# Moving every large on-chip tile to a multiple of 512 bytes, and keeping only gelu's slope, in a two-layer decode training step

## The chip, the cores and the metric

The kernel runs on one NeuronCore of a Trainium2 chip. The metric is the device time of one execution in microseconds (us); lower is better. Of the core, five instruction streams matter here: TensorE (PE, with its weight loads shown apart as PEld), VectorE (DVE), ScalarE (ACT), GpSimd (POOL) and SyncE (SP). SP and POOL issue the transfers between main memory (HBM) and the on-chip memory (SBUF); 16 DMA engines carry them out. SBUF has 128 partitions; a tile has the same byte offset in every one of them.

## The reference

Forward and backward pass of four blocks for two rows of 1,024 numbers: attention with a cached context, MLP, and the same two again with the same weights. The inputs are bfloat16.

```
def _A_ref(x, k_cache, v_cache, wq, wo):      # caches [2, 4, 16384, 128], 32 query heads, 8 to a cache head
    q = (x @ wq) in heads
    p = _softmax(q . k_cache * Dh ** -0.5)
    return (p . v_cache) in heads joined @ wo
def _B_ref(x, w1, b1, w2, b2):                # w1 [1024, 3584], w2 [3584, 1024]
    y = _layernorm(x)
    h = _gelu(y @ w1 + b1)                    # tanh form of gelu
    return h @ w2 + b2
x = A_x
x = x + _A_ref(_layernorm(x), ...)            # layer 0
x = x + _B_ref(_layernorm(x), ...)
x = x + _A_ref(_layernorm(x), ...)            # layer 1
x = x + _B_ref(_layernorm(x), ...)
```

Returned are the output and the gradients of A_x, of both caches, and of wq, wo, w1, b1, w2 and b2 for a given gradient of the output. The caches are 32 MB each and are read several times; their gradients are as large and are written once, for both layers together.

## The kernel before

**What streams.** Two rows leave almost no reuse, so the kernel is a stream of 1 MB chunks from HBM. A chunk is a slot tile of 128 partitions by 8,192 bytes: a quarter of one cache head's keys or values (8,192 bytes in a row), or four 128-row blocks of a weight matrix (four runs of 2,048 bytes), or one block of w1 (7,168 bytes). There are 14 slot tiles, and three more slots in the tile `last` until the last stage; the halves of tiles that are not yet in use (`e1`, `ds1`) serve as slots for a while.

**Order.** Pieces of work are recorded with `emit` in the order in which they are to run, each with the chunks that it uses. `Program.run` goes through them once, gives a chunk a slot as soon as one is free, issues its load on SP's queue (L288 for caches, L293 for weights) and frees the slot behind the last piece that uses it. Nothing is reordered after that: the order on each engine is the order of the pieces.

**Stages.** Attention of layer 0 (`attn_fwd`), MLP forward of layer 0 (`mlp_in`, `w1_fwd`, `gelu_fwd`, `gelu_out`, then w2), attention and MLP of layer 1, the MLP backward of layer 1, attention backward of layer 1 (`attn_bwd`), MLP backward of layer 0, attention backward of layer 0 with all the weight and cache gradients. In an attention stage PE turns 128x128 blocks of a chunk (L321), ACT or DVE copies eight turned blocks from PSUM into one of three tiles `kT` (L191, L194), and PE multiplies by them (L661 forward, L937 backward). Other blocks are used as they are loaded (L644, L918). In the last stage the gradients are made in PSUM (L1022, L1069), copied by ACT or DVE (L199, L202) into a half slot, the staging buffer, and stored by POOL (L1029, L1085) in pieces of 512 KB, 4,096 bytes to a partition.

**gelu.** `gelu_fwd` (L734 to L754) makes from the sums of w1 the tiles `hpre` (the input of gelu), `sg` (one over 1 + e^z), `gq` (1 - sg, the sigmoid) and `pl` (the polynomial in the slope), each 128 partitions by 56 numbers, 224 bytes, and keeps all four per layer in the pool `vec`. `gelu_out` makes gelu from `gq` and `hpre` for the w2 product. `gelu_slope` (L760 to L766) turns `pl` into gelu's slope with three DVE instructions:

```
        V.tensor_tensor(out=pl[:], in0=pl[:], in1=sg[:], op=ALU.mult)
        V.tensor_scalar(out=pl[:], in0=pl[:], scalar1=1.0, scalar2=None, op0=ALU.add)
        V.tensor_tensor(out=pl[:], in0=pl[:], in1=q[:], op=ALU.mult)
```

For layer 1 it is called right behind `gelu_fwd` (L1189). For layer 0 it is called in the MLP backward of that layer (L1258), ahead of the seven pieces `w2_use` and the multiplication at L1263 that needs it.

**Where tiles lie.** The pools lie one behind the other in each partition, in the order in which they are opened: `const`, `vec`, `wrk`, `small`, `ktp` (the three `kT`), `pers` (`e0`, `e1`, `ds1`, `last`, then the 14 slots). A tile's size is rounded up to 32 bytes. So a byte added to an early pool moves all that lies behind it. Adding the sizes up, the first `kT` begins at byte 32,672, the first slot at byte 114,592, and the last slot ends at byte 229,280.

Of the kernel before, what the change touches and what calls it, by code (L numbers as in the profile page):

```python
# [9 lines left out]
F32 = mybir.dt.float32  # L10
I32 = mybir.dt.int32
ACT = mybir.ActivationFunctionType
ALU = mybir.AluOpType
# [10 lines left out]
LAG_B = 13  # L24
LAG_K = 15
NSTG = 12
STG_FROM = (0, 0, 0, 4, 8, 12)


# [23 lines left out]
class Program:  # L53
# [11 lines left out]
    def emit(self, fn, uses=()):  # L65
        i = len(self.ops)
        self.ops.append((fn, tuple(uses)))
        for c in uses:
            if c.first is None:
                c.first = i  # L70
            c.last = i
# [31 lines left out]
def kernel(  # L103
# [25 lines left out]
    V = nc.vector  # L129
# [11 lines left out]
    FJ = F // 128  # L141
# [8 lines left out]
    emit = P.emit  # L150
# [5 lines left out]
    const = ctx.enter_context(tc.tile_pool(name="const", bufs=1))  # L156
    vec = ctx.enter_context(tc.tile_pool(name="vec", bufs=1))
    wrk = ctx.enter_context(tc.tile_pool(name="wrk", bufs=2))
# [62 lines left out]
    ones_all = const.tile([128, 128], BF16, name="ones_all")  # L221
    V.memset(ones_all[:], 1.0)
    sel8 = const.tile([16, 8, 128], BF16, name="sel8")
    ident_d = dram.tile([128, 128], BF16, name="ident_d")


# [15 lines left out]

    stg_used = [0] * NSTG

    def staging():

        i = min((i for i in range(NSTG) if P.now >= marks[f"bwd0 {STG_FROM[i // 2]}"]), key=lambda i: stg_used[i])
        stg_used[i] = st["stg"] = st["stg"] + 1
# [20 lines left out]
    dh_all = vec.tile([128, FJ, 4], BF16, name="dh_all")  # L269
# [33 lines left out]
    def ld_w1():  # L303
        return [ld_rows(B_w1, j, 1, 0, F) for j in range(DJ)]

    def ld_w2():
        return [ld_rows(B_w2, 4 * i, 4, 0, D) for i in range(FJ // 4)]
# [372 lines left out]
    def w1_fwd(l, ws, then=lambda j: ()):  # L680

        hps = half[0, 0][:, 0:FJ * 2].rearrange("p (j b) -> p j b", b=2)
        emit(lambda: V.memset(hps, 0.0))
        for j in range(DJ):
            def f(j=j):
                for o in range(FJ):
                    PE.matmul(hps[:, o, :], lhsT=col(ws[j], 0, F, o), rhs=m_all[:, j, 2 * l:2 * l + 2],
                              start=False, stop=True, skip_group_check=True)
            emit(f, [ws[j]])
            for p in then(j):  # L690
                emit(*p)
        return hps
# [39 lines left out]

    def gelu_fwd(l, hps):

        hpre = vec.tile([128, FJ, 2], F32, name=f"hpre{l}")
        V.tensor_tensor(out=hpre[:], in0=hps, in1=b1T[:].to_broadcast([128, FJ, 2]), op=ALU.add)
        x2 = wrk.tile([128, FJ, 2], F32, name="g_a", bufs=1)
        V.tensor_tensor(out=x2[:], in0=hpre[:], in1=hpre[:], op=ALU.mult)
        u = wrk.tile([128, FJ, 2], F32, name="g_b", bufs=1)
        V.tensor_scalar(out=u[:], in0=x2[:], scalar1=GELU_A, scalar2=1.0, op0=ALU.mult, op1=ALU.add)  # L740
        V.tensor_tensor(out=u[:], in0=u[:], in1=hpre[:], op=ALU.mult)
        z = wrk.tile([128, FJ, 2], F32, name="g_c", bufs=1)
        S.activation(out=z[:], in_=u[:], func=ACT.Exp, scale=2.0 * GELU_C)

        pl = vec.tile([128, FJ, 2], F32, name=f"pl{l}")
        V.tensor_scalar(out=pl[:], in0=x2[:], scalar1=6.0 * GELU_A * GELU_C, scalar2=2.0 * GELU_C, op0=ALU.mult,
                        op1=ALU.add)
        V.tensor_tensor(out=pl[:], in0=pl[:], in1=hpre[:], op=ALU.mult)
        V.tensor_scalar(out=z[:], in0=z[:], scalar1=1.0, scalar2=None, op0=ALU.add)
        sg = vec.tile([128, FJ, 2], F32, name=f"sg{l}")  # L750
        V.reciprocal(out=sg[:], in_=z[:])
        q = vec.tile([128, FJ, 2], F32, name=f"gq{l}")
        V.tensor_scalar(out=q[:], in0=sg[:], scalar1=-1.0, scalar2=1.0, op0=ALU.mult, op1=ALU.add)
        saved[f"gelu{l}"] = (hpre, q, sg, pl)  # L754

    def gelu_out(l):
        hpre, q = saved[f"gelu{l}"][:2]
        V.tensor_tensor(out=h_all[:, :, 2 * l:2 * l + 2], in0=q[:], in1=hpre[:], op=ALU.mult)

    def gelu_slope(l):  # L760

        hpre, q, sg, pl = saved[f"gelu{l}"]
# [3 lines that stand above are left out]
        return pl  # L766
# [384 lines left out]
    xA0 = attn_fwd(0, up, lambda: xT0, kept(keep0, Kv, "K"), kept(keep0, Vv, "V"))  # L1151
    chain(lambda: mlp_in(0, xA0), 2)
    hps = w1_fwd(0, ld_w1())
    emit(lambda: (gelu_fwd(0, hps), gelu_out(0)))
    ws2 = ld_w2()
    fps = half[0, 1][:, 0:DJ * 2].rearrange("p (j b) -> p j b", b=2)
    dhps = sb[0][:, 0:FJ * 2].rearrange("p (j b) -> p j b", b=2)
# [29 lines left out]
    def turn_round():  # L1187
        gelu_fwd(1, hps1)
        d1 = gelu_slope(1)  # L1189
        V.tensor_tensor(out=dh_all[:, :, 2:4], in0=d1[:], in1=dh_last[:], op=ALU.mult)  # L1190
        gelu_out(1)
# [54 lines left out]
    dhps0 = half[0, 1][:, 0:FJ * 2].rearrange("p (j b) -> p j b", b=2)  # L1246
# [7 lines left out]
                              stop=(o == DJ - 1))  # L1254
        return f, [ws2c[i]]

    slope0 = {}
    emit(lambda: slope0.setdefault("d", gelu_slope(0)))  # L1258
    for i in range(FJ // 4):
        emit(*w2_use(i))  # L1260
        for p in w1_turned(ws1c, i, ws1c[i], act=False) if 1 <= i < 6 else ():
            emit(*p)
    emit(lambda: V.tensor_tensor(out=dh_all[:, :, 0:2], in0=slope0["d"][:], in1=dhps0, op=ALU.mult))  # L1263
    for j in (6, 7):
        for p in w1_turned(ws1c, j, ws1c[j], act=False):
            emit(*p)
# [53 lines left out]

    slots = [Slot(t[:], until=marks[f"bwd0 {STG_FROM[i]}"] if i < len(STG_FROM) else None) for i, t in enumerate(slot_tiles)]
    slots += [Slot(last_t[:, i * CH:(i + 1) * CH], until=marks["bwd0 0"]) for i in range(3)]
# [35 lines left out]
```

## Time and profile before

| | |
|---|---|
| device time, median of 3 runs | 1207.09 us (1203.09 to 1207.83) |
| device time of the profiled execution | 1211.49 us |
| its span, first to last instruction | 1209.6 us |
| mean granted TensorE clock | 0.858 of full speed |
| HBM read, written | 352.37 MB, 98.62 MB |
| DVE busy | 605.5 us (50%) |
| ACT busy | 555.2 us (46%) |
| POOL busy | 125.1 us (10%) |

The span is what the profile's times count in; the device time is 1.9 us more in the profiled execution. In the profile, L191 is line 191 of the kernel, `kT<-tp` says that tile `kT` is written from tile `tp`, and buffer numbers are left out. Issues of transfers are not counted as busy time. The DMA share of a stretch is the summed time of the packets that began in it over 16 engines' time; packets overlap a little, so a full stretch shows about 1.02.

### The profile page before, as it was taken

The numbers are of one execution on the slowest core, as the hardware profiler recorded it, in microseconds if no ns is written. First come the engines' busy times: TensorE is split into PE (matmuls) and PEld (weight loads), VectorE is DVE, ScalarE is ACT, GpSimd is POOL, SyncE is SP. The second block draws the span as 40 slices with busy tenths as digits, with TensorE's granted clock in tenths as the row PEclk, the third lists the DMA queues.
The fourth block names the chain that finished last, engine by engine and source line by source line (L and its number), as shares of the span: only waits on it lengthen the run. The fifth ranks groups of instructions, "written<-read, shape, count | busy, mean of one in ns | idle before, by whom it ended". The sixth has DMA issues, their size and how long they took to land. (4 is left out here: it accounts for less than half of the span.)

```text
span 1209.6 us, 44046 instructions
## 1 busy us (share of the span) xinstructions
PE 1036.5 (86%) x19762; PEld 864.8 (71%) x19805; DVE 605.5 (50%) x1266; ACT 555.2 (46%) x996; POOL 125.1 (10%) x214
## 2 busy tenths in 40 slices
PE   6878896689898988888988988988988899799996
PEld 6867885588888888888988977555555556556663
DVE  2423242134333323433433443877866787677875
ACT  1423241124333423333433433767766677677774
POOL 1000000000000000000000010322222222222222
PEclk8967586579877757898889987999988999999998
DMA  9999999989999996999999886899998999999995
GB/s 357 412 413 413 413 413 412 382 281 372 413 413 417 414 391 265 394 411 410 408 374 325 321 311 244 323 367 373 411 416 311 386 414 418 379 394 411 417 413 197
DMA packets 106041, 453.83 MB, mean 375 GB/s; under 512 B 8658, under 2 KB 8658, under 8 KB 75516
## 3 DMA queue, kind: packets, MB, share of 16 engines
q1 hardware_dynamic: 78780, 352.36, 74.3%
q0 software_dynamic: 27072, 98.66, 20.3%
q8 instruction: 154, 2.52, 0.8%
q14 instruction: 35, 0.29, 0.1%
HBM read 352.37 MB, written 98.62 MB: 373 GB/s over the span
## 5 line engine op out<-in xcount | busy, mean ns | idle before, releaser
L191 ACT COPY kT<-tp 128x512 int32<-128x512 int32 x427 | 250.4, 586 | 428.1 <-PE tp L321 399.9
L321 PE MATMUL tp<-ident,slot 128*128 128x128 bf16 x4224 | 368.6, 238 | 12.6 <-issue 7.1
L321 PEld LDWEIGHTS <-slot 128*128 128x128 bf16 x4224 | 284.2, 107 | 29.8 <-issue 12.8
L194 DVE COPY kT<-tp 128x1024 bf16<-128x1024 bf16 x209 | 144.5, 691 | 302.7 <-PE tp L321 257.0
L199 ACT CAST slot<-sc 128x512 bf16<-128x512 f32 x271 | 157.8, 589 | 51.7 <-PE sc L1022 18.9
L202 DVE CAST slot<-sc 128x512 bf16<-128x512 f32 x227 | 154.3, 688 | 39.2 <-PE sc L1022 17.5
L1022 PE MATMUL sc<-last 128*128 128x512 bf16 x324 | 119.6, 387 | 19.6 <-ACT slot L199 5.3
L918 PEld LDWEIGHTS <-slot 128*128 128x128 bf16 x1888 | 80.5, 98 | 43.1 <-issue 18.8
L937 PEld LDWEIGHTS <-kT 128*128 128x128 bf16 x2048 | 80.8, 97 | 37.7 <-issue 20.5
L1029 POOL DMA_DIRECT2D out_dram<-slot x128 | 69.0, 539 | 281.7 <-ACT slot L199 174.8
L202 DVE CAST slot<-sb 128x512 bf16<-128x512 f32 x126 | 86.7, 688 | 17.6 <-PE sb L1022 6.4
L661 PE MATMUL sc<-qd,kT 128*128 128x8 bf16 x2048 | 90.7, 171 | 3.6 <-issue 3.5
L937 PE MATMUL sc<-qd,kT 128*128 128x8 bf16 x2048 | 89.9, 170 | 1.0 <-issue 0.8
L199 ACT CAST slot<-sb 128x512 bf16<-128x512 f32 x128 | 75.4, 589 | 28.6 <-PE sb L1069 16.0
L661 PEld LDWEIGHTS <-kT 128*128 128x128 bf16 x2048 | 73.2, 99 | 4.1 <-issue 3.9
L1022 PE MATMUL sb<-last 128*128 128x512 bf16 x161 | 61.9, 384 | 6.6 <-ACT slot L199 1.6
L362 PE MATMUL tp<-ident,slot 128*128 128x128 bf16 x692 | 58.6, 239 | 6.9 <-issue 2.9
L644 PE MATMUL sb<-e,slot 128*128 128x8 bf16 x1280 | 56.7, 176 | 8.3 <-ACT e L580 3.5
L1069 PE MATMUL sc<-last 128*128 128x512 bf16 x155 | 56.4, 383 | 4.8 <-DVE last L1057 3.4
L644 PEld LDWEIGHTS <-slot 128*128 128x128 bf16 x1280 | 50.2, 102 | 11.9 <-issue 7.6
L362 PEld LDWEIGHTS <-slot 128*128 128x128 bf16 x692 | 48.3, 108 | 12.4 <-issue 9.8
L191 ACT COPY slot<-tp 128x512 int32<-128x512 int32 (+1 forms) x52 | 29.8, 574 | 52.5 <-PE tp L362 52.1
(292 smaller groups left out, 1270.9 us busy)
## 6 DMA issues: line engine op xcount, KB each, us to landing
slot<-in_A_k_cache_dram SPq DMA_DIRECT2D x101, 1024.0 KB, 10.1
slot<-in_A_v_cache_dram SPq DMA_DIRECT2D x91, 1024.0 KB, 12.0
out_dram<-slot POOLq DMA_DIRECT2D x182, 512.0 KB, 10.5
slot<-in_A_wq_dram SPq DMA_DIRECT2D x28, 1024.0 KB, 9.7
slot<-in_A_wo_dram SPq DMA_DIRECT2D x23, 1024.0 KB, 16.2
last<-in_A_v_cache_dram SPq DMA_DIRECT2D x16, 1024.0 KB, 15.0
slot<-in_B_w_dram SPq DMA_DIRECT2D x18, 896.0 KB, 13.9
slot<-in_B_w_dram SPq DMA_DIRECT2D x12, 1024.0 KB, 12.2
```

Source lines behind the costliest of these rows:

```text
L191: S.copy(out=dst.bitcast(I32), in_=src.bitcast(I32))
L194: V.tensor_copy(out=dst, in_=src)
L199: S.copy(out=dst, in_=src)
L202: V.tensor_copy(out=dst, in_=src)
L321: PE.transpose(tp[:, j, :], t, ident[:])
L362: PE.transpose(tp[:, j, :], t, ident[:])
L644: PE.matmul(acc, lhsT=c.ap[:, ((vi % 4) * 8 + j) * 128:((vi % 4) * 8 + j + 1) * 128], rhs=e[:, vi, :, j], start=(vi == 0 and j == 0), stop ...
L661: PE.matmul(sc[t // 64][:, :, t % 64], lhsT=kT[:, j, :], rhs=qd[:, 0, g, l, :], start=True, stop=True)
L918: PE.matmul(sb[0][:, 0:8], lhsT=c.ap[:, ((vi % 4) * 8 + j) * 128:((vi % 4) * 8 + j + 1) * 128], rhs=d[:, vi, :, j], start=(vi == 0 and j = ...
L937: PE.matmul(scb[0][t // 64][:, :, t % 64], lhsT=kT[:, j, :], rhs=qd[:, 1, g, l, :], start=True, stop=True)
L1022: PE.matmul(ps, lhsT=hold["blk"][:, 2 * (hc % 2) + u // 2, :], rhs=flat(qms[w][:, (u % 2) * 4:(u % 2) * 4 + 4, :]), start=True, stop=True)
L1029: GP.dma_start((dKv if w == 0 else dVv)[g, :, hc * 16:(hc + 1) * 16, :], stg.rearrange("p (t d) -> p t d", d=128))
```

## The change

A constant `PAD = 192` and a tile of 128 partitions by 192 bytes that nothing reads or writes are added at the end of the pool `const`. In `gelu_fwd` three of the four kept tiles go to scratch: `hpre` to a new scratch tile `g_h`, `sg` into `g_b` (which held the argument of the exponential) and `gq` into `g_a` (which held the square). Only `pl`, now named `slope`, stays in `vec`. Since scratch is written again by the other layer, layer 0's `gelu_slope` moves from the MLP backward to right behind `gelu_out(0)` in the MLP forward.

```
@@ -24,6 +24,7 @@
 NSTG = 12
+PAD = 192
 STG_FROM = (0, 0, 0, 4, 8, 12)
@@ -221,6 +222,8 @@
     sel8 = const.tile([16, 8, 128], BF16, name="sel8")
+
+    const.tile([128, PAD // 4], F32, name="pad")
     ident_d = dram.tile([128, 128], BF16, name="ident_d")
@@ -732,7 +735,7 @@
     def gelu_fwd(l, hps):
-        hpre = vec.tile([128, FJ, 2], F32, name=f"hpre{l}")
+        hpre = wrk.tile([128, FJ, 2], F32, name="g_h", bufs=1)
...
-        pl = vec.tile([128, FJ, 2], F32, name=f"pl{l}")
+        pl = vec.tile([128, FJ, 2], F32, name=f"slope{l}")
...
-        sg = vec.tile([128, FJ, 2], F32, name=f"sg{l}")
+        sg = wrk.tile([128, FJ, 2], F32, name="g_b", bufs=1)
         V.reciprocal(out=sg[:], in_=z[:])
-        q = vec.tile([128, FJ, 2], F32, name=f"gq{l}")
+        q = wrk.tile([128, FJ, 2], F32, name="g_a", bufs=1)
@@ -1151,7 +1154,8 @@
     hps = w1_fwd(0, ld_w1())
-    emit(lambda: (gelu_fwd(0, hps), gelu_out(0)))
+    slopes = {}
+    emit(lambda: (gelu_fwd(0, hps), gelu_out(0), slopes.setdefault(0, gelu_slope(0))))
@@ -1254,13 +1258,11 @@
-    slope0 = {}
-    emit(lambda: slope0.setdefault("d", gelu_slope(0)))
     for i in range(FJ // 4):
         emit(*w2_use(i))
...
-    emit(lambda: V.tensor_tensor(out=dh_all[:, :, 0:2], in0=slope0["d"][:], in1=dhps0, op=ALU.mult))
+    emit(lambda: V.tensor_tensor(out=dh_all[:, :, 0:2], in0=slopes[0][:], in1=dhps0, op=ALU.mult))
```

No other instruction moves on any engine, and every transfer keeps its place on its queue.

## The prediction

> **What bounds the kernel now.** I read the page first: its forty slices of DMA and its queues.
>
> ```profile
> DMA  9999999989999996999999886899998999999995
> GB/s 357 412 413 413 413 413 412 382 281 372 413 413 417 414 391 265 394 411 410 408 374 325 321 311 244 323 367 373 411 416 311 386 414 418 379 394 411 417 413 197
> DMA packets 106041, 453.83 MB, mean 375 GB/s; under 512 B 8658, under 2 KB 8658, under 8 KB 75516
> q1 hardware_dynamic: 78780, 352.36, 74.3%
> q0 software_dynamic: 27072, 98.66, 20.3%
> ```
>
> The DMA engines are nearly always busy, and in about half of the slices the rate sits on one plateau, 410 to 418 GB/s. The busy shares of the two data queues add to 94.6% of the span. TensorE is second. The same in stretches of 30 us shows where which of them limits (columns: stretch, length, busy us of PE, PEld, DVE, ACT, POOL, clock, DMA share, GB/s):
>
> ```profile
> 60.00:90.00 30.00, 21.38 (x451) 20.27 (x450) 7.17 (x17) 7.45 (x14) 0.00 (x0) 0.69 1.02 412
> 210.00:240.00 30.00, 16.84 (x393) 16.01 (x394) 4.82 (x23) 3.18 (x6) 0.72 (x1) 0.52 1.00 383
> 540.00:570.00 30.00, 25.02 (x588) 24.56 (x587) 11.04 (x30) 11.14 (x19) 0.00 (x0) 0.88 1.02 410
> 660.00:690.00 30.00, 27.08 (x660) 26.23 (x657) 12.34 (x27) 12.31 (x21) 0.00 (x0) 0.94 0.85 315
> 750.00:780.00 30.00, 27.44 (x336) 16.93 (x334) 24.52 (x41) 23.02 (x43) 9.23 (x14) 0.99 0.71 265
> 1140.00:1170.00 30.00, 28.05 (x450) 19.34 (x454) 22.85 (x42) 20.66 (x39) 6.40 (x12) 1.00 1.03 418
> ```
>
> Of the forty such stretches 27 have a DMA share of 0.99 or more (30 to 240, 300 to 450, 480 to 600, 810 to 900, 930 to 1170): 810 us, in which 329 MB of the 453.8 MB move, 73%. There a shorter packet is a shorter kernel. In the others (the start, 240 to 300, 450 to 480, 600 to 810, 900 to 930, the end) PE, or the copies behind it, set the pace.
>
> So the question is what a packet costs, and whether the start address is part of that. The trace's records of single packets, by size, with the commonest and the mean duration:
>
> ```
> queue            bytes   packets   commonest ns   mean ns
> q1 loads          2048     39941             84      90.0
> q1 loads          7168      3073            272     288.2
> q1 loads          8192     30336            309     324.7
> q0 stores         4096     23296            159     162.2
> q0 stores         6144       512            234     239.4
> q0, semaphores       4      3180              9       9.0
> ```
>
> The commonest durations go up by 75 ns for each 2,048 bytes: 84, 159, 234, 309. That is 27.3 bytes per ns and engine, 437 GB/s for 16, plus 9 ns a packet. Packet time therefore splits into 453.83 MB / 437 = 1,039 us of moving bytes, 97,158 data packets x 9 ns / 16 = 55 us of fixed time, and the excess of the means over the commonest values, (6.0 x 39,941 + 16.2 x 3,073 + 15.7 x 30,336 + 3.2 x 23,296 + 5.4 x 512) / 16 = 53 us of stalls. Successive packets overlap: the start that follows a packet's end most often lies 3 to 4 ns ahead of that end, so only some 5 ns of the 9 cost time, 32 us in all.
>
> **The change part by part.**
>
> *The addresses.* `const` gains 192 bytes, `vec` loses six tiles of 224 (1,344 bytes), `wrk` gains one of 224: all from `kT` on moves down by 928 bytes. The first `kT` was at 32,672 = 63 x 512 + 416, and is now at 31,744 = 62 x 512. `kT` tiles, `e`, `ds1`, slots, half slots and the parts of `last` are all multiples of 512 long, so all of them were at 416 past a multiple of 512 and are now on one. That is also 160 past a multiple of 256 and 32 past a multiple of 64. Among each other they keep their distances, so no two of them meet in a new way.
>
> *What a packet can gain.* The moving of bytes: nothing, since every size already runs on the one line of 27.3 bytes per ns. A penalty for each block of 64, 256 or 512 bytes would make that line steeper than the rate of the loads that differ in row length, and it does not. The fixed part: the lower bound is nothing, because the 4-byte semaphore packets, which have no row to be split, pay the same 9 ns. So do loads (address shift on the written side) and stores (shift on the read side), which speaks for a cost that is not the shift. The upper bound is all of the 5 ns that count, 32 us. I take 1 ns a packet: the records come in steps of about 2 ns (7, 9, 11, 13), so one block less to touch in 9, 17 or 33 would not be seen in them. 97,158 x 1 / 16 = 6.1 us, of which 73%, 4.4 us, lies in full stretches. The stalls: between nothing and all 53 us, 39 us in full stretches. I take nothing: 4,096-byte stores lose 3 ns and 2,048-byte loads 6 although both are shifted alike, and 8,192-byte loads lose most of their 16 ns in 1,061 packets of 30,336 that took over 15% longer, which looks like waiting for memory and not like a tax on every packet.
>
> The Trainium skill ("DMA: Bandwidth & Descriptors", How a descriptor splits into AXI transactions) says that a transaction must start at a multiple of 256 bytes, and that the bytes from that boundary to the descriptor's start are fetched unused. At a shift of 160 bytes this would cost each store 160 / 27.3 = 5.9 ns, 23,808 x 5.9 / 16 = 8.8 us by an estimate from that page, and the loads, which read from HBM, nothing. The rows do not bear it out: stores and loads have the same 9 ns.
>
> *The engines.* PE reads the moved tiles, ACT and DVE write them. Is there a row that depends on the address? `ones_all` lies on a multiple of 64, the slots and `kT` lie 32 past one, and their weight loads of the same shape take (minimum/median/maximum ns):
>
> ```profile
> L589 PEld LDWEIGHTS <-ones_all x32: 97/98/151, 41.9 to 436.9; 128*128 128x128 bf16 x32
> ```
>
> ```profile
> L321 PEld LDWEIGHTS <-slot x4224: 95/98/293, 12.4 to 1166.3; 128*128 128x128 bf16 x192
> ```
>
> ```profile
> L937 PEld LDWEIGHTS <-kT x2048: 95/96/152, 490.2 to 1171.7; 128*128 128x128 bf16 x187
> ```
>
> No difference beyond 2 ns. I take zero; the bounds are minus and plus 2 ns on the 6,765 weight loads of the stretches where DMA isn't full, 13.5 us either way. For ACT and DVE copies no row has another address (586 and 691 ns throughout); in full stretches they have slack (DVE 11 us of 30), and I take zero with those same bounds.
>
> *gelu's slope.* Three DVE instructions, 0.20 + 0.19 + 0.22 = 0.61 us (0.67 with the gaps between them), leave 704.8 us and come in at 233.95. Where they leave:
>
> ```profile
> 704.81 0.20 DVE L763 TENSOR_TENSOR pl<-pl,sg 128x56 f32<-128x56 f32 x1
> 705.04 0.19 DVE L764 TENSOR_SCALAR pl<-pl 128x56 f32<-128x56 f32 x1
> 705.26 0.22 DVE L765 TENSOR_TENSOR pl<-pl,gq 128x56 f32<-128x56 f32 x1
> 706.06 1.29 DVE L194 COPY slot<-tp 128x1024 bf16<-128x1024 bf16 x2 [0.58 <-PE tp L362]
> ```
>
> The copy behind them waits 0.58 us longer for PE, so their removal frees nothing. Where they come in, the queue behind them on DVE is the memset of L1158, which moves from 233.95 to about 234.6. PE first needs it for the w2 sums, after two chunks of four turned blocks, several us later; DVE's next copy comes behind 4.2 us of waiting for PE, and the stretch has DMA share 1.00. Cost: nothing; without that cover, 0.67 us. Layer 1 runs the same instructions on other tiles. `g_b` is overwritten behind ACT's exponential, which L749 already waits for, and `g_a` behind a reader on DVE itself: no new wait.
>
> Sum: 4.4 us off the profiled execution's 1211.5 us, 1207.1. The median of the runs shown is 4.4 us lower than that execution, so 1207.1 - 4.4 = 1202.7, say 1203.
>
> **Rivals.**
>
> *The stalls were due to the shift* (faster). For it: stalls exist, 53 us, 48 of them in loads, whose written side is shifted. Against it: stores stall less with the same shift, and most loads of 8,192 bytes are within 5 ns of the commonest value. No row decides between none and all; with half of the loads' 48 us gone, 24 x 0.73 = 17.5 us, the time is 1190.
>
> *TensorE reads slower from the new addresses* (slower). The place is the stretches that DMA does not fill, above all 600 to 810 us. At the 2 ns that the rows leave open, not hidden, the cost is 13.5 us: 1207 + 13.5 = 1221. From 0.9 ns per weight load (6 us) it makes the kernel measurably slower. Against it are the three medians above.
>
> *The change doesn't reach what it names*: if HBM's side alone shapes the packets, the address on chip is without effect and the time stays at 1207.
>
> **How the numbers follow.** A difference of 0.5%, 6 us, is about what can be told from no change here; the three runs spread over 4.7 us. The forecast (0 to 2 ns a packet, 1198 to 1208) gets 0.50, of which 0.13 lies beyond 6 us. The stalls get 0.28 (1165 to 1198; all faster), slower reads 0.14 (1208 to 1225; 0.13 of it slower), no effect 0.08. Faster 0.41, same 0.46, slower 0.13. The range from 1183 to 1213 leaves out about a tenth at either end: more than two thirds of the stalls gone, or more than half of the 2 ns on the weight loads.
>
> **What would show it.** Commonest packet durations of 83 and 308 ns or less where there were 84 and 309, means falling with them, plateaus of 412 to 418 GB/s moving up by 1 to 5; PE's and the copies' medians unchanged; L763 to L765 right behind L758 at about 234 us, no wait of PE behind them. If the means fall and the commonest values stay, the stalls were the shift's. If LDWEIGHTS medians move, or the 600 to 810 us part gets longer, the rival on TensorE holds. The prediction is wrong if the plateaus move by more than 2%, or if the gain appears where DMA isn't full.

## The result, and the profile after

| | before | after |
|---|---|---|
| device time, median of 5 runs | 1207.09 us (1203.09 to 1208.33) | 1194.48 us (1192.82 to 1198.63) |
| ratio, 95% interval | | 0.9899 [0.9867, 0.9930] |
| span of the profiled execution | 1209.6 us | 1192.7 us |
| mean granted TensorE clock | 0.858 | 0.864 |

The kernel is 1.0% faster: by the ratio 12.2 us, interval 8.4 to 16.1. The forecast was 1203 (1183 to 1213). The two profiled executions lie 16.9 us apart, more than the medians, because the one shown of before was 4.4 us slower than its median. Medians and ratios are of executions at the usual clock; one execution of the kernel "slots shifted" below took 1280.75 us at a clock of 0.625 and is left out of them.

The page of the kernel after, DMA in forty slices and its queues:

```profile
DMA  9999999989999996999999976899999999999994
GB/s 365 420 421 421 422 420 421 386 298 378 420 420 420 422 409 264 378 414 418 417 402 330 365 295 232 323 376 373 417 417 373 384 417 410 371 362 409 416 415 200
DMA packets 106041, 453.83 MB, mean 381 GB/s; under 512 B 8658, under 2 KB 8658, under 8 KB 75516
q1 hardware_dynamic: 78780, 352.36, 74.5%
q0 software_dynamic: 27072, 98.66, 20.5%
```

Same packets, same bytes. The plateau in the first half, where almost only loads run, went from 412 to 414 up to 420 to 422. In the last third, where loads and stores run together, it hardly moved. The same in longer stretches that DMA fills, before:

```profile
60.00:200.00 140.00, 114.20 (x2471) 108.56 (x2474) 41.77 (x95) 41.69 (x73) 0.00 (x0) 0.71 1.02 414
1080.00:1150.00 70.00, 64.86 (x944) 42.50 (x948) 55.85 (x94) 50.56 (x93) 17.82 (x32) 1.00 1.02 415
```

and after:

```profile
60.00:200.00 140.00, 116.10 (x2489) 110.57 (x2495) 43.60 (x101) 41.55 (x74) 0.00 (x0) 0.68 1.02 421
1080.00:1150.00 70.00, 64.70 (x976) 43.38 (x982) 54.46 (x95) 49.87 (x92) 16.77 (x30) 1.00 1.02 417
```

Where in the kernel the time went is read from two instructions that occur once for each layer: the first of gelu (first and last start in the MLP forward of layer 0 and of layer 1) and the last addition of an attention backward (layer 1, then layer 0 near the end). Before:

```profile
L736 DVE TENSOR_TENSOR hpre<-sc,b1T x2: 205/210/216, 231.5 to 468.3; 128x56 f32<-128x56 f32 x2
L965 DVE TENSOR_TENSOR gA<-lb_dx,g x2: 174/174/174, 703.3 to 1189.7; 128x16 f32<-128x16 f32 x2
```

After:

```profile
L739 DVE TENSOR_TENSOR g_h<-sc,b1T x2: 206/210/215, 227.2 to 458.9; 128x56 f32<-128x56 f32 x2
L968 DVE TENSOR_TENSOR gA<-lb_dx,g x2: 174/174/174, 686.0 to 1173.0; 128x16 f32<-128x16 f32 x2
```

The gain grows through the three stages of loads, 4.3, 9.4 and 17.3 us, and the last stage, with the stores, takes as long as before: 486.4 and 487.0 us. One pair of executions exaggerates this. Over the six profiled executions with shifted slots and the four with the slots on a multiple of 256 (this pair and the kernels below), the same three marks gain 3.2, 7.1 and 12.9 us in the mean, and the last stage takes 484.3 and 485.9 us.

What changed in a packet? Over the whole kernel the commonest durations did not. What changed is how many packets have them (short stalls: up to 15% above the commonest duration; long ones: beyond; summed over the kernel and divided by 16 engines):

```
                        commonest   mean          at commonest   short stalls   long stalls
                               ns   ns            duration       us             us
2048-byte loads  before        84   90.0           59%            4.7           10.3
                 after         84   88.0           97%            0.0            9.9
8192-byte loads  before       309   324.7          38%            6.3           23.5
                 after        309   322.2          94%            0.7           24.4
4096-byte stores before       159   162.2          85%            1.5            3.2
                 after        159   161.5          93%            0.4            3.2
```

With the 7,168-byte loads, the short stalls of loads went from 11.5 us to 0.8, a saving of 10.7 us. The long ones are what they were, 36.5 and 37.2 us.

The packets by stage show more than the sums. Of the 11.5 us of short stalls before, 4.3, 8.1 and 10.9 us lie ahead of the three marks above, and only 0.5 us past 740 us, where loads and stores run together (0.5 in the kernel after, too). From 60 to 200 us, where only loads run, 29% of the 2,048-byte and 10% of the 8,192-byte loads had the durations of 84 and 309 ns before, and 100% and 99% have them after. In that stretch the commonest duration of an 8,192-byte load was 311 ns before, and the means fell from 87.8 to 84.4 and from 315.6 to 310.6 ns. The 309 ns in the table is commonest before only because the last stage is in it.

TensorE and the copies did not move: weight loads from slots have a median of 98 ns on the old address and the new, those from `kT` 96.

```profile
L324 PEld LDWEIGHTS <-slot x4224: 94/98/292, 12.3 to 1149.7; 128*128 128x128 bf16 x192
```

```profile
L940 PEld LDWEIGHTS <-kT x2048: 95/96/152, 480.4 to 1155.0; 128*128 128x128 bf16 x187
```

And gelu's slope runs where the prediction put it, ahead of the memset, with DVE idle behind it:

```profile
229.53 0.21 DVE L766 TENSOR_TENSOR slope<-slope,g_b 128x56 f32<-128x56 f32 x1
229.78 0.19 DVE L767 TENSOR_SCALAR slope<-slope 128x56 f32<-128x56 f32 x1
230.00 0.22 DVE L768 TENSOR_TENSOR slope<-slope,g_a 128x56 f32<-128x56 f32 x1
230.23 0.07 DVE L1162 MEMSET sc<- 128x16 f32 x1
233.28 0.69 DVE L195 COPY kT<-tp 128x1024 bf16<-128x1024 bf16 x1 [2.98 <-PE tp L324]
```

### The profile page after: what moved, and what is told of

Same layout as the page of the kernel before. It is cut to its first block, busy times and chain, and to the rows that moved or that the text cites. A ratio compares the mean times of both kernels' runs of the same rounds, so it can differ in the third digit from the quotient of the medians.

```text
span 1192.7 us, 44045 instructions
## 1 busy us (share of the span) xinstructions
PE 1032.3 (87%) x19762; PEld 859.1 (72%) x19805; DVE 605.4 (51%) x1266; ACT 554.8 (47%) x996; POOL 125.1 (10%) x214
## 5 line engine op out<-in xcount | busy, mean ns | idle before, releaser
L365 PEld LDWEIGHTS <-slot 128*128 128x128 bf16 x692 | 48.2, 107 | 11.5 <-issue 9.0
## 6 DMA issues: line engine op xcount, KB each, us to landing
slot<-in_A_wq_dram SPq DMA_DIRECT2D x28, 1024.0 KB, 10.7
```

Of the source, the lines that this page charges most:

```text
L365: PE.transpose(tp[:, j, :], t, ident[:])
```

## Experiments

### Which part of the change, and which tiles

Theory A says that the on-chip address which a load writes costs the short stalls. Its rivals: gelu's part (B), and the engines' own reads and writes at the shifted address (C). Four kernels take the change apart.

The address without gelu's part and without a pad. This is the kernel before, with 416 bytes less in front of `kT`:

```
-    wrk = ctx.enter_context(tc.tile_pool(name="wrk", bufs=2))
+    wrk = ctx.enter_context(tc.tile_pool(name="wrk", bufs=1))
...
-                gm = small.tile([8, 1], F32, name="gm")
+                gm = small.tile([8, 1], F32, name="gm", bufs=2)
```

> The kernel before, with no pad and gelu as it was; the slots, staging and kT come to a multiple of 512 bytes only because six scratch tiles of wrk are single and one small tile is double instead of triple (416 bytes less in front of them; the order and the waits on every engine stay). Theory A (the start address of what the loads write costs short stalls in each packet): about 1195 us, ratio 0.990; the mean of 2,048-byte loads 88.0 ns and of 8,192-byte loads about 322 ns, pure-load stretches at 420 GB/s. Theory B (gelu's shorter keeping, not the address): about 1207, ratio 1.00, means 90.0 and 325.

gelu's part without the address:

```
-PAD = 192
+PAD = 96
```

> The changed kernel with PAD = 96 instead of 192: gelu's slope made early, but every large tile again at 416 past a multiple of 512. Theory A: 1207, ratio 1.00, means 90.0 and 325 ns, pure-load stretches at 413 GB/s. Theory B: 1195, ratio 0.99.

Only `kT` shifted (the pad of 96, and 96 bytes more behind the `kT` tiles):

```
-PAD = 192
+PAD = 96
...
+    pers.tile([128, 24], F32, name="pad2")
     Et = [pers.tile([128, G * 1024], BF16, name=f"e{l}") for l in range(2)]
```

> The changed kernel with the kT tiles (written by ACT and DVE, read by PE, never touched by a transfer) back at 416 past a multiple of 512, and everything from e0 on, slots too, on a multiple of 512. Theory A (address of what transfers write): 1195, ratio 0.990, load means 88 and 322 ns. Theory C (the engines' own reads and writes at the shifted address): most or all of the gain gone, 1203 to 1207.

Only the buffers of transfers shifted, `kT` not:

```
+    pers.tile([128, 104], F32, name="pad2")
     Et = [pers.tile([128, G * 1024], BF16, name=f"e{l}") for l in range(2)]
```

> The changed kernel with kT on a multiple of 512, and e0, e1, ds1, last and all slots, so every buffer of a load or a store, at 416 past one. Theory A: 1207, ratio 1.00, load means 90 and 325 ns. Theory C with kT as the place: 1195, ratio 0.99, load means 88 and 322 ns only if the engines disturb the transfers.

Measured, with the kernel before on the same chip at 1208.73 us ("at": bytes past a multiple of 512):

| kernel | slots at | kT at | median us | ratio, 95% interval | short stalls of loads us |
|---|---|---|---|---|---|
| address alone | 0 | 0 | 1193.78 | 0.9875 [0.9836, 0.9914] | 0.6 |
| gelu alone | 416 | 416 | 1205.73 | 0.9977 [0.9953, 1.0000] | 11.2 |
| kT shifted | 0 | 416 | 1195.80 | 0.9896 [0.9863, 0.9928] | 2.0 |
| slots shifted | 416 | 0 | 1209.92 | 0.9996 [0.9970, 1.0021] | 11.2 |

All of the gain goes with the address of the slots and the other buffers of transfers. Theory B falls, and C for `kT`. The engines read and write the slots too, so whether their accesses are needed for the cost is left to the kernels that only transfer. gelu's part alone is within half a percent of no change: it made room for the pad, and that is all that it can be shown to do. The load stretch from 60 to 200 us, of the kernel with the address alone:

```profile
60.00:200.00 140.00, 115.00 (x2518) 108.71 (x2525) 43.59 (x101) 42.52 (x75) 0.00 (x0) 0.73 1.02 421
```

and of that with only the slots shifted:

```profile
60.00:200.00 140.00, 115.11 (x2467) 110.08 (x2470) 41.30 (x94) 41.70 (x73) 0.00 (x0) 0.69 1.02 414
```

### Which multiple

The change goes to multiples of 512 bytes. Four kernels place all tiles 32, 64, 128 and 256 bytes past one:

```
-PAD = 192
+PAD = 224     # then 256, 320, 448
```

> The changed kernel with PAD = 224: every large tile 32 bytes past a multiple of 512. What decides is the size of the block that a load's write must begin on. Block of 32 bytes or none: 1195 us. Block of 64, 128, 256 or 512: 1206 (ratio 0.998), load means 90 and 324 ns, pure-load stretches 413 GB/s.

> PAD = 256: 64 bytes past a multiple of 512. Block of 64: the whole gain, 1195 us (0.990), 88 and 322 ns, 421 GB/s. Block of 128, 256 or 512: 1206, 90 and 324 ns, 413 GB/s.

> PAD = 320: 128 bytes past a multiple of 512. Block of 64 or 128: 1195 us and 421 GB/s. Block of 256 (the Trainium skill, DMA: Bandwidth & Descriptors, How a descriptor splits into AXI transactions, has transactions of 256 bytes that begin on multiples of 256) or 512: 1206 and 413 GB/s.

> PAD = 448: 256 bytes past a multiple of 512. Block of 64, 128 or 256: 1195 us and 421 GB/s. Block of 512, as the change has it: 1206 and 413 GB/s.

| past a multiple of 512 by | median us (before: 1209.26) | ratio, 95% interval | short stalls of loads us |
|---|---|---|---|
| 32 | 1209.51 | 1.0009 [0.9989, 1.0028] | 13.2 |
| 64 | 1209.36 | 1.0008 [0.9976, 1.0040] | 11.2 |
| 128 | 1207.46 | 1.0005 [0.9982, 1.0028] | 10.5 |
| 256 | 1193.07 | 0.9898 [0.9867, 0.9929] | 1.0 |

Of the time it is all or nothing, and the step is at 256: of the starts tried (32, 64, 128, 256 and 416 bytes past a multiple of 512) only the multiples of 256 have the gain; 512 is more than is needed. This agrees with the Trainium skill ("DMA: Bandwidth & Descriptors", How a descriptor splits into AXI transactions), whose transactions are 256 bytes long and begin on multiples of 256. That section gives its cost for a read that begins off such a place; here it is the written side of a load. The row with PAD = 448:

```profile
60.00:200.00 140.00, 113.82 (x2534) 106.64 (x2530) 44.36 (x102) 42.72 (x75) 0.00 (x0) 0.76 1.02 421
```

### Transfers alone

Does the shift cost something by itself, or only where engines use the same memory? The next kernel (it and the two that follow ran once each) issues transfers and nothing else, between HBM and twelve tiles that begin on multiples of 512:

```
for what, count in ((caches, 32), (weights, 32), (stores, 64)):
    for shift in (0, 160, 256, 32):              # bytes into the tile
        what(shift, count)                       # loads on SP's queue, stores on POOL's
```

> Transfers alone, with PE, ACT, DVE idle: nothing of the reference is computed, one output is written with loaded data. Twelve stages: 32 cache loads (8,192-byte runs) with the slots at 0, 160, 256 and 32 past a multiple of 512; then 32 weight loads (2,048-byte runs) at the same four; then 64 stores (4,096-byte runs) from the same four. If the short stalls belong to the transfer itself, loads at 0 and 256 run near 421 GB/s with over 90% of packets at 309 and 84 ns, and at 160 and 32 near 413 with 40 to 60%. If they come from the engines' reads and writes of the same memory, all four are alike near 421. Stores: alike at all four, near 418, if reading at a shift is free; 3 to 4% slower at 160 if each fetches from the 256-byte boundary below (an estimate from the Trainium skill, DMA: Bandwidth & Descriptors, How a descriptor splits into AXI transactions: 5.9 ns on 159).

Its stretches, one for each kind and shift, cache loads at 0, 160, 256 and 32, then weight loads at the same, then stores at the same. (Columns: stretch, length, POOL's busy time, clock, DMA share, GB/s.)

```profile
20.00:85.00 65.00, 0.00 (x0) 1.00 1.01 428
105.00:155.00 50.00, 0.00 (x0) 1.00 1.01 422
180.00:240.00 60.00, 0.00 (x0) 1.00 1.01 428
260.00:310.00 50.00, 0.00 (x0) 1.00 1.01 421
340.00:400.00 60.00, 0.00 (x0) 1.00 1.05 409
420.00:480.00 60.00, 0.00 (x0) 1.00 1.05 387
505.00:575.00 70.00, 0.00 (x0) 1.00 1.05 408
600.00:625.00 25.00, 0.00 (x0) 1.00 1.04 387
695.00:740.00 45.00, 18.09 (x34) 1.00 1.02 409
770.00:815.00 45.00, 17.54 (x33) 1.00 1.00 384
845.00:910.00 65.00, 26.87 (x52) 1.00 1.02 412
940.00:985.00 45.00, 18.22 (x35) 1.00 0.99 382
```

The cost belongs to the transfer, and theory C falls for the slots too: no engine computes here. Loads of 8,192-byte runs lose 1.5%, of 2,048-byte runs 5.4%, stores of 4,096-byte runs 6 to 7%. In these stretches, loads at a shift of 160 have means of 313.9 ns instead of 309.0 and 88.6 instead of 84.0, and at 32 they have 314.5 and 88.2. So a run that does not begin on a multiple of 256 costs 4 to 6 ns in the mean, at 2,048 bytes as at 8,192. The kernel's own stretch of loads agrees, with 3.4 and 4.9 ns. The rates expected for loads (421 against 413 GB/s) were missed: 8,192-byte runs are faster at every shift, and 2,048-byte runs slower.

Stores at 160 and at 32 have means of some 169 ns, instead of 161 at 256 (163 at 0). The expectation for stores was missed: not free, as their commonest duration in the kernel had seemed to say. By the estimate from the Trainium skill ("DMA: Bandwidth & Descriptors", How a descriptor splits into AXI transactions) the cost is proportional to the shift, 5.9 ns at 160 and 1.2 ns at 32. Measured are some 8 ns at both, against the starts on 256.

The second such kernel shifts the HBM side, the on-chip side, or both:

```
for what, count in ((loads, 32), (stores, 64)):
    for there, here in ((0, 0), (160, 0), (0, 160), (160, 160)):
        what(there, here, count)                 # runs of 7680 and 3584 bytes
```

> Transfers alone again, nothing computed, one output partly written. Loads of 7,680-byte runs with (HBM side, on-chip side) at (0, 0), (160, 0), (0, 160), (160, 160) past a multiple of 256; then stores of 3,584-byte runs at the same four. Theory A, the written address alone: the loads at (0, 160) and (160, 160) are slower than at (0, 0) by 1 to 2%, those at (160, 0) are not; the stores at (160, 0) and (160, 160), whose write into HBM is shifted, are slower. Theory D, the two sides must have the same place in a block: (160, 160) is as fast as (0, 0), and both (160, 0) and (0, 160) are slow. Theory E, the read side costs too: (160, 0) is slower for loads and (0, 160) for stores.

Loads, then stores, in the order of the list:

```profile
25.00:70.00 45.00, 0.00 (x0) 1.00 1.02 427
90.00:140.00 50.00, 0.00 (x0) 1.00 1.02 427
165.00:210.00 45.00, 0.00 (x0) 1.00 1.02 422
235.00:280.00 45.00, 1.50 (x3) 1.00 1.02 422
...
330.00:380.00 50.00, 23.06 (x43) 1.00 1.01 405
395.00:450.00 55.00, 25.66 (x48) 1.00 1.00 396
470.00:525.00 55.00, 24.75 (x46) 1.00 1.00 386
545.00:595.00 50.00, 22.06 (x41) 1.00 0.99 380
```

For loads it is theory A to the letter: 160 bytes of shift on the HBM side cost nothing (427 GB/s), on the on-chip side they do (422), and shifting both alike doesn't help, so D falls. For stores both sides cost, 2% on the HBM side and 5% on the chip's: A alone does not cover them, part of E holds.

### Why the last stage gained nothing

If stores alone lose 6% and loads 1.5%, the last stage should have gained most. It gained nothing. Either the cost vanishes where loads and stores alternate, or TensorE and the copies pace the stage.

```
for stage, shift in enumerate((0, 160, 256, 32)):
    for i in range(60):
        loads(shift, mine, i)                    # six tiles, SP's queue
        stores(shift, other, i)                  # the other six, POOL's queue
```

> Transfers alone, loads (8,192-byte runs) and stores (4,096-byte runs) at the same time from separate tiles, as in the kernel's last stage, at 0, 160, 256 and 32 past a multiple of 512; nothing is computed, one output is written with loaded data. The kernel's last stage gained nothing from the new addresses, though loads alone lose 1 to 2% and stores alone 5% at a shift of 160. Theory F (where loads and stores take turns, the shift's cost lies under the other's transfer): all four stages run at the same rate within 1%, and loads keep 309 ns. Theory G (the cost stays, and the last stage gained nothing because TensorE and the copies pace it): the stages at 160 and 32 are 2 to 4% slower than those at 0 and 256.

The four stages, in that order:

```profile
40.00:220.00 180.00, 23.94 (x45) 1.00 1.02 425
260.00:430.00 170.00, 24.23 (x46) 1.00 1.02 425
470.00:640.00 170.00, 24.61 (x47) 1.00 1.02 425
690.00:870.00 180.00, 28.06 (x53) 1.00 1.02 425
```

Theory F: one rate at every shift, with 99% and more of the packets at 309 and 159 ns. Where as many loads as stores are under way (6,224 and 6,223 packets in the first stretch), a shifted start is free, and the two together run better than stores alone at any address (409 to 412 GB/s). The kernel's own last stage agrees: past 740 us, 95% and 83% of its 2,048-byte and 8,192-byte loads were at 84 and 309 ns before, and 96% and 84% after. Its stores lost 1.1 us of short stalls (1.5 to 0.4), which its length does not show. So the last stage had nothing to gain. How one transfer covers the other inside the DMA engine, no run here shows.

## Why the prediction was right, and where it was not

**The number.** The range held, but not through the forecast's mechanism. 1194.5 lies outside the 1198 to 1208 us of the forecast and inside the 1165 to 1198 of the rival on stalls, which had 0.28; the range reached down into that rival, to 1183. The forecast's own step towards faster came from the fixed part, which did not shrink, so that it pointed the right way was luck. The plateaus of loads rose by 7 to 8 GB/s, 1.9%, not by 1 to 5, just short of the 2% that the prediction named as its own refutation.

**What bounds the kernel.** Right: a shorter packet was a shorter kernel. In six executions with shifted slots the attention backward of layer 1 ends at 701.4 to 704.7 us, 702.8 in the mean; in four with the slots on a multiple of 256 at 686.0 to 696.3, 689.9 in the mean. That is 12.9 us, about the 10.7 us of short stalls; the difference is less than the spread. Between the second and the third mark above the mean gain grows by 5.9 us, though only 2.8 us of short stalls lie there; no run here says whether that is chance.

**The fixed part, "I take 1 ns a packet".** Wrong, with its reason: 4.4 us were expected from 1 ns less in every packet, loads and stores alike. The commonest durations stayed at 84, 159 and 309 ns over the whole kernel. Nor do the records come in steps of 2 ns: the transfers alone have packets of 84, 85 and 86 ns.

**The stalls, "I take nothing".** This is the step that failed. The term was 0 and measured 10.7 us of packet time in loads; the 1.1 us that went from stores lie in the last stage, which got no shorter. The rival that the stalls were the shift's was the true mechanism. Its price, half of the loads' 48 us, gave 1190 where 1194.5 was measured; in truth it was nearly all of the 11.5 us of short stalls and none of the 36.5 us of long ones.

Two readings led away from it. The commonest value of a distribution is that of the packets which did not pay: 41% of the 2,048-byte loads and 62% of the 8,192-byte loads lay above it. And "most loads of 8,192 bytes are within 5 ns of the commonest value" was held against the rival, though 5 ns is just the cost, 1.6% of a packet. Split by stage, the same record of before would have told: 311 ns where only loads run, 309 where stores run too. That stores and loads share the 9 ns of fixed time was no evidence on the shift either.

**"4,096-byte stores lose 3 ns and 2,048-byte loads 6 although both are shifted alike."** The stores were measured where they alternate with loads, and there the cost is hidden.

**The Trainium skill's rule on 256-byte starts** (the section named above). It was set aside because the rows showed no 5.9 ns on stores. Its block of 256 was right, and the store alone does pay, some 8 ns; the rows had been taken from a stage that hides it.

**TensorE and the copies at zero, gelu's slope at zero.** Right: medians of 98 and 96 ns as before (the 6,765 of the bound counts matmuls; weight loads are 6,745, which leaves the 13.5 us), copies of 586 and 691 ns as before, `kT` shifted or not within each other's intervals (0.9896 and 0.9875), and gelu alone 0.9977 with an interval that reaches 1.

**Full stretches, 73%.** The wrong cut. What counted was which stretches carry loads without stores: 11.1 of the 11.5 us of short stalls lie ahead of 740 us.

## What to carry to other kernels

Begin every on-chip run that a load writes on a multiple of 256 bytes; adding up the tiles ahead of it tells whether it does, and a few bytes of pad or of freed scratch mend it. The shorter the contiguous run, the more it is worth: in streams of loads alone 5% at 2,048 bytes and 1.5% at 8,192, and nothing where as many stores ran beside 8,192-byte loads. Judge a transfer by the whole distribution of its packets, in a stage where nothing covers it, and not by the commonest value.

## What was not expected of the hardware

- A shifted start costs a load 4 to 6 ns for each run, 32 bytes past the multiple as much as 160 (314.5 and 313.9 ns on 8,192 bytes, 88.2 and 88.6 on 2,048).
- Loads and stores together moved 425 GB/s, stores alone 412 at best, 8,192-byte loads alone 428.
- With the engines idle, loads on a multiple of 256 ran with practically every packet at its commonest duration. The 36 to 37 us of long stalls that the kernel has before and after are not in those stages. Their cause stays open.
